# State scalings over all 128 partitions with a zero-padded scale table, and another order of work, in a retention and channel-mixer kernel

## The chip, the cores and the metric

The kernel runs on one core of one Trainium2 chip. The metric is the device time of one execution in microseconds (us), as the median of several runs; lower is better. A profile of one execution is read beside it. In the profile PE is the TensorE matmul engine, PEld its weight loads, DVE is VectorE, ACT is ScalarE, POOL is GpSimd and SP is SyncE, whose queue here only issues DMAs. "L434" is line 434 of the kernel file. In the changed file the same statements stand one or two lines further down.

## The reference

Two parts follow each other. The first is a retention layer: for each of 4 batches and 8 heads a 64x64 state decays by a constant gamma of the head at every one of 768 time steps, takes in an outer product of k and v, and is read by q. The second is a mixer over tokens and then over channels, with relu in between.

```python
def _attn_ref(q, k, v) -> np.ndarray:
    B, H, S, D = q.shape                      # 4, 8, 768, 64
    gamma = 1.0 - 2.0 ** (-5.0 - np.arange(H, dtype=np.float32))
    scale = 1.0 / np.sqrt(D)
    for t in range(S):
        state = gamma[None, :, None, None] * state + np.einsum('bhd,bhe->bhde', k[:, :, t], v[:, :, t])
        y[:, :, t] = scale * np.einsum('bhd,bhde->bhe', q[:, :, t], state)

def _moe_ref(x, w_tok1, w_tok2, w_ch1, w_ch2) -> np.ndarray:
    xt = x.transpose(0, 2, 1)
    h = np.maximum(xt @ w_tok1, 0.0) @ w_tok2        # 768 -> 256 -> 768
    u = x + h.transpose(0, 2, 1)
    h2 = np.maximum(u @ w_ch1, 0.0) @ w_ch2          # 512 -> 1536 -> 512
    return (u + h2).astype(np.float32)
```

## The kernel before

Time is cut into 6 chunks of 128 steps, and heads are taken in 4 pairs per batch, so that a pair fills 128 partitions (64 rows for each head). Work falls into a "front" for each batch and pair, and a "back" for each batch.

A front loads k, q and v of the pair by DMA, scales k and q by decays (L343 on ACT or L345 on DVE), turns them (PE transposes at L377 and L379, or DMA transposes issued by SP at L367, with the evictions L387 and L392), and forms two things. Scores within a chunk come from PE at L453 and are masked by DVE at L463 into the tile `am`. States between chunks come from PE at L408 into a bank, and DVE runs the recurrence over the five chunk ends at L418 and L420 into the tile `U` (128 partitions, 5 blocks of 64). The state is then scaled once more by the pair's decay over a chunk and written, as f16, into a tile `diag`, of 5 blocks of 128x128 that hold head 0 in the upper left quarter and head 1 in the lower right one, and zeros elsewhere (L434 on ACT, L436 on DVE; one instruction for each head). With it one full matmul per chunk (L483) serves both heads. PE adds both parts in a bank (L474 and L483), ACT or DVE evicts it (L489, the cast `x`), the token mixer follows (L503, relu at L512 or L514, L523), and the result is cast (`u`, L529), kept in f32 (`X`, L539) and turned into `uT` (PE at L568 with the eviction L575 for the first batch, and a DMA transpose issued by SP at L553 for the others).

A back does the channel mixer of a batch: `widen` (L606, relu at L622) and `narrow` (L746), or variants that save one product in eight by sums of blocks (L679 with evictions L691, L696 and L717; L820 and L830 with evictions L810 and L837, and sums at L784). Outputs leave at L761 and L862.

The three buffers of `diag` are one constant tile. It is set to zero once by a DVE memset (L233), and the scalings write only the diagonal quarters:

```python
rows = rows_of(j)                                   # 64 rows of head j
r, u, g = RS.tile[rows, :, rows], US.tile[rows], gp[rows, p:p + 1]
if e == "ACT":
    nc.scalar.activation(r, u, AF.Copy, scale=g)    # L434
else:
    nc.vector.tensor_scalar(r, u, g, None, ALU.mult)  # L436
```

`gp` holds the decay of pair p in column p, head 0 on partitions 0 to 63 and head 1 on the others, by eight memsets (L229, L230).

The order is a table. `PLAN` is a string that names, one after the other, each operation of the program, with the engine on which it runs where two can do it, and the PSUM bank that it takes; "+" and a digit stand for that many filler matmuls on a tile of zeros (L935), which compute nothing that is used. `placed` reads it, and each engine gets its instructions in that order. Engines run their queues in order and wait for each other by semaphores. DMAs of the POOL and SP queues are issued in the table's order too.

Of the kernel before, what the change touches and what calls it, by code (L numbers as in the profile page):

```python
# [8 lines left out]
FP = mybir.dt.float32  # L9
F16 = mybir.dt.float16  # L10
AF = mybir.ActivationFunctionType
ALU = mybir.AluOpType
# [9 lines left out]
class Op:  # L22
# [15 lines left out]
DIGITS = "0123456789abcdefghijklmnopqrstuvwxyzABCDEFGHIJKLMNOPQRSTUVWXYZ"  # L38

PLAN = (  # L40
    "0500040b0f01080702030d1h10a1i0+e1n01o1j1060e0h1p1q1k0+31l2091m+51w211z1v340c1y1r0g1S01T01s+61U41t01W01Y21u01V0"
    "1x1A1X+32x11Z0i2t026042021280j27352u0+62v02b1B52w0221C2y230m1E62401F250292a2z21D00k1G00l2H012J2K2A2B2c42C2D"
    "+12d2f32E2F12g+11H11I1J00n2I022L0p2M2N10r2e02h02G01N1K2i01L02j2k13412O1M02Q20q1O02R351385390E0w2P02l2S01P00o"
    "3602o2m03a63b3703c2T53d2U3e2n03i073k3L42V03f2p02q02W3j053l3g02r33o72Z3h03p1Q63n0t3m0u3M1R13r02X03003s3253q03t0"
    "2s03310x3u43v3H03w14k64l3114T50s5s44U3I03x3y02Y0aD33A3D2aA65t3B03J53F3E0aBaJ1aKaE3K13z13G0bj5aC3C00zaFaL3N7"
    "3V06243Z0v0Aba3bkbbbcb443Wbg03XbH1bIb5bE3bhbi3Y3O0y4g13PbF3Q3R4h10C3SbJb12b2b34i03T1431b77b8b6bG0D0Bbl4P14j1"
    "4u04260H4Q14xaY34w4R53U0aZaG2b0b9aS4aHaI444v0G40741aT4y4m24S14V5421466451bv347aV04W4n4Xbw480494c4o4paU0F4Y4q4Z"
    "4rbx500I19aP45353264a0aW4d14b0aM754aNaQ4z5555105204s04t11faO0Jbm3bnbd7aX4AaRbs456btbB2bKbp04e04B0by1bqbobCbzbr"
    "bebfbD4F01a575b65c4C3154DbM164E04f587bQ2171cbLbu4G4H00P595o15a0bO44IbA5d04LbP04J05e15f186114M0bR5p1bT5q2c6bN"
    "5u00K5v5g05w4K1bU05h5k5x5r0cc15i0ca55y5zbXcdc8bY10L4N05Y05Z05j05l05m060bV15C70325A0bW5G646655F0M5n5B0620bZc263"  # L50
    "5K3cb0ch266c74O0N7G05D5Ecfcs5L5H05I5J00Rcy7c0cuc3ci676869ctcvcg07H15M0cw15N45Ocj5P05Q5Tck00Oczc95R0cD45S06x1cl"
    "cocm1dce5U0cp5V0cE5W3cx06y0cB6D26EcC06FbS5X06c5076cHcF6dd356A1cI6B0cG0di47607820Q6g6a16zcO36C6GcP0ScU6cQcVd4"
    "6b1df3djdgd5dhcK6fd956e7716HdV3cJcW0VcL6h6dWd61d7dadb7a0dl01e6Idm6J16K17b17I26i6k5do26ldn1gdS7dTd00dpd86j06m0"
    "6n17c6o1bcndk6p1dqdXdUd1dx2dyd2dz6L71347K06P6N7d00W79du26tdv6q6O7L16r0cX1dD36M8k0dc4dd7edE6s1dF6u16v0de7f7g6T6"
    "6U7hc1dM7cY6Q3dw6R0U0TcR5cScAcZcTdYdN7N16S07i7OdZ7PdP2e06V0dQ6W56X6Y08l1dJ07MdKdLdO7J8Q1dR7Q7R7S726ZdG5700710"
    "7307j1dHdI7408g07T08R0e278h0e310X6w0Y7l12047oe437U07k0e7e57m7p8m7ne96eadr18Tds7V24307We817q57Z8jed7t2118S28i2"
    "dt7rdA17udBee7s0eb7v0dC7w6ec07x7y07Ye1eg8367X80481ef84eh8X7820eG8n17z7C863ek8U08508V1878YeI8o8Z7A0eM07B08808W"
    "898p7D090eNel8q7E08a0eK38ceq2eR0138b0eL0en8r8d0918s929308v7145eHeS8xer7FePeQ08w8yeVeW8t0eo28zemeO8e0ep0eT8u0et"
    "eu0eU1955064758f8A78Be6ex998C08D49697esey09q0ev1eweX8EeC9409r08F0eDez12eJeAf210cM1c41cq1fB0f62f78G58Hf3a00eB"
    "8I00ZeYfk1fCa22f85fafFc50f5eZflfof9fD3fbfGfd8Jfm59u0fp9v1cN0fI8Ma11fEfJf4frfc39wfe98fn8K0fq6fffsfy9a5fNcr0fO9t"  # L60
    "fifwfj14fgft9ba39c09s19d09efhfu9f1f11g62fvfAfxg79g3ei1eE19h8N09x19i09ya768L09za89Agaa9gk39j8O09BaafH4glgm79mgo"
    "9CfKgbabgnfLg81fP79k09l09n09o0fMacgpgd9F6405g9fz9Jgc1fQgefTgigrf00gq59G9D09HfR6fV49IfU9E09K09LgffSgjgs9M09N2fW"
    "fXgggtgy9Ogw9Q69P0gu9Ra41a50fYghad0g1fZg3gva6g4g09S09W9Tgx9U0gAg59V09X0g2gz8PgBgCgF3gXeF0h14gH0gG0af7561gDgIah"
    "gKh209Y0gM2agh30gL0ae0gNajgZgOak79palgYgQh81gP0am0aian6aogEgJap1h6aq5h0h9argT9Zh70as0atau0awgRhjh4gSh5haax0az"
    "hb0gUhlav0hchp0hfhu3hkhdhehvhFhJ1hKhn7hX5hYho1hqhh0ay0hyhGej1hshHi1hL6hZ0hghrhMhzie4ht0hwi2hx0hmi4hNhOig3hAi0"
    "hBhIhQhP0ifhRiiis6i32hSihi5hVi6hTichCijhWi9iahUi7iJ1itiy3iliX0i8ik2imiu5iYiwj1inioj2ixidipiKiqiZ7ibj0irj4iviz"
    "j5iL2iNj34iP5iMjbiOj9gW0hE1gV1iQiAjW2iEhi1iRj6iBj7jaiSiCkc0iTiFiGiDiIiVjcj8iUjdiHiWjejAjgjE3jF0ji6jXjYjZk0k1"
    "jG5jCjBhD0jL4jp1jJjj0jMjfjnjK0jNjo0jPjHjDk2jqjIk30jQjrjO0jSjRjtjU1jTkdk43kekfjV0js1kgkhjujvjhjk1jy1jwk5k6kijl"
    "kj0jmk7k8jxk9kajz0kb0"
)  # L70


# [24 lines left out]
def kernel(  # L97
# [11 lines left out]
    nc = tc.nc  # L109
    B, H, S, D = q.shape  # L110
# [58 lines left out]
    def either(emit, **costs):  # L169
        return [(e, c[0], c[1], lambda emit=emit, e=e: emit(e)) for e, c in costs.items()]  # L170
# [62 lines left out]
    diag_op = prep("DVE", 775, lambda: nc.vector.memset(diag, 0.0), prio=(-20, 0, -1, 2))  # L233
# [80 lines left out]
    def front(b, p):  # L314
# [19 lines left out]
        def rows_of(j):  # L334
            return slice(j * D, (j + 1) * D)
# [90 lines left out]
        for j in range(2):  # L426
            def emit(e, j=j):
                if RS.tile is None:
                    RS.tile = diag[:, rcount[0] % BUFS["r16"]]
                    rcount[0] += 1  # L430
                rows = rows_of(j)
                r, u, g = RS.tile[rows, :, rows], US.tile[rows], gp[rows, p:p + 1]
                if e == "ACT":
                    nc.scalar.activation(r, u, AF.Copy, scale=g)  # L434
                else:
                    nc.vector.tensor_scalar(r, u, g, None, ALU.mult)  # L436
# [531 lines left out]
```

## Time and profile before

| what | us |
|---|---|
| median of 3 runs | 188.86 (187.83 to 189.07) |
| the profiled execution, its own time | 187.85 |
| its span, first to last instruction | 186.1 |
| DVE busy, all of the span | 162.8 |
| ACT busy | 125.8 |
| POOL busy | 38.8 |
| granted TensorE clock | 1.00 throughout |

The span leaves out 1.75 us of the execution's own time. The busy time of an engine is the union of its instructions; matmuls overlap each other in the pipeline, so the distance from one matmul to the next says more than the duration of one. The prediction shows the rows that it uses.

### The profile page before, as it was taken

Reading aid. Unit: us, or ns where it says so; the run is one execution under the profiler, and the core shown is the slowest. Engines: PE = TensorE matmul, PEld = TensorE weight load, DVE = VectorE, ACT = ScalarE, POOL = GpSimd, SP = SyncE. Lnnn points to the kernel's source line nnn. Section 1 sums busy time; section 2 is a strip of 40 time slices with the busy share of each in tenths; the row PEclk is TensorE's granted clock in tenths of the full one; section 3 lists DMA queues with packets and bytes.
Section 4 is the critical chain, followed back from the end, with each engine's and each line's share of the span. In section 5 each row is a group of like instructions: output and inputs, shape, how many; then the busy total and the mean of one; then the engine's idle time right before and its main releaser. Section 6 shows DMA issues by size and latency. Waiting matters only on the chain.

```text
span 186.1 us, 5220 instructions
## 1 busy us (share of the span) xinstructions
PE 179.2 (96%) x2079; PEld 135.2 (73%) x2079; DVE 162.8 (88%) x424; ACT 125.8 (68%) x288; POOL 38.8 (21%) x49
## 2 busy tenths in 40 slices
PE   7889999899999999999999999999999999999993
PEld 3556888567679898667677888767678987656882
DVE  5589889689999999995889899989999999789882
ACT  3768898654969948557789677889986435774100
POOL 8994199373015000101003000010000000000000
PEclk9999999999999999999999999999999999999999
DMA  8999999999999999399999799979528031231044
GB/s 114 151 166 202 175 184 185 167 193 206 179 154 158 148 113 224 79 176 230 228 181 138 176 168 216 309 191 226 194 45 187 0 99 62 86 139 58 4 181 157
DMA packets 94233, 29.05 MB, mean 156 GB/s; under 512 B 84352, under 2 KB 91264, under 8 KB 94208
## 3 DMA queue, kind: packets, MB, share of 16 engines
q0 software_dynamic: 39520, 9.64, 54.1%
q1 hardware_dynamic: 52816, 15.93, 47.5%
q10 hardware_dynamic: 1872, 3.15, 4.7%
q8 instruction: 16, 0.26, 0.6%
q14 instruction: 9, 0.07, 0.2%
HBM read 26.74 MB, written 6.29 MB: 178 GB/s over the span
## 4 chain that ended last, share of the span: by engine, by line
PE 81%; ACT 7%; DVE 4%; DMA 3%; POOL 2%; issue 1%; POOLq 0%; DVEq 0%; ACTq 0%
PE bank L820 16%; PE bank L606 15%; PE bank L679 15%; PE bank L830 12%; PE bank L503 5%; PE bank L523 5%; DMA row<-in_k_dram 3%; PE bank L453 3%; PE bank L746 3%; PE bank L474 3%; PE bank L483 2%; ACT diag L434 2%; DVE am L463 2%; PE bank L408 1%; DVE U L420 1%; ACT X L539 1%
## 5 line engine op out<-in xcount | busy, mean ns | idle before, releaser
L606 PE MATMUL bank<-uT,wc 128*128 128x384 f16 x192 | 36.3, 326 | 0.7 <-ACT uT L575 0.6
L463 DVE TENSOR_TENSOR am<-bank,mask 128x384 f16<-128x384 f32 x64 | 32.8, 550 | 3.9 <-PE bank L453 3.7
L622 ACT ACTIVATE h<-bank 128x384 f16<-128x384 f32 x48 | 21.3, 497 | 9.5 <-PE bank L606 9.3
L606 PEld LDWEIGHTS <-wc 128*128 128x128 f16 x192 | 17.4, 98 | 9.8 <-issue 0.9
L696 DVE TENSOR_TENSOR h<-bank,us 128x384 f16<-128x384 f32 x36 | 19.1, 552 | 2.4 <-PE bank L679 1.6
L691 ACT COPY us<-bank 128x384 f32<-128x384 f32 x36 | 16.4, 487 | 6.6 <-PE bank L679 5.1
L820 PEld LDWEIGHTS <-hs 128*128 128x128 f16 x198 | 18.8, 98 | 2.6
L837 DVE TENSOR_TENSOR X<-X,bank 128x256 f32<-128x256 f32 x44 | 18.0, 415 | 2.4 <-PE bank L830 2.1
L810 ACT COPY us<-bank 128x256 f32<-128x256 f32 x27 | 10.1, 380 | 14.1 <-PE bank L820 13.1
L820 PE MATMUL bank<-wsum,hs 128*128 128x256 f16 x132 | 17.5, 273 | 0.0
L420 DVE SCALAR_TENSOR_TENSOR U<-U,gp,bank 128x64 f32<-128x64 f32 x64 | 16.4, 276 | 0.9
L360 POOL CAST v<-row 128x768 f16<-128x768 f32 x5 | 4.1, 827 | 61.5 <-DMA row<-in_v_dram 53.0
L529 ACT CAST u<-bank 128x384 f16<-128x384 f32 x30 | 14.6, 499 | 2.7 <-PE bank L523 2.6
L489 ACT CAST x<-bank 128x384 f16<-128x384 f32 x28 | 12.9, 485 | 3.7 <-PE bank L483 3.5
L679 PE MATMUL bank<-hs,wsum 128*128 128x384 f16 x72 | 15.3, 326 | 0.0
L523 PE MATMUL bank<-h,wt 128*128 128x128 f16 x192 | 14.5, 219 | 0.0
L503 PE MATMUL bank<-x,wt 128*128 128x128 f16 x192 | 14.2, 219 | 0.2 <-ACT x L489 0.2
L539 ACT COPY X<-bank 128x384 f32<-128x384 f32 x28 | 14.0, 503 | 0.1
L434 ACT ACTIVATE diag<-U,gp 64x320 f16<-64x320 f32 x24 | 13.3, 559 | 0.9 <-DVE U L420 0.4
L830 PEld LDWEIGHTS <-h 128*128 128x128 f16 x132 | 12.3, 98 | 1.8
L503 PEld LDWEIGHTS <-wt 128*128 128x128 f16 x192 | 12.0, 98 | 2.1 <-issue 0.6
L523 PEld LDWEIGHTS <-wt 128*128 128x128 f16 x192 | 12.1, 98 | 1.9 <-issue 0.2
(91 smaller groups left out, 364.3 us busy)
## 6 DMA issues: line engine op xcount, KB each, us to landing
out_dram<-X SPq DMA_DIRECT2D x12, 256.0 KB, 2.8
out_dram<-X ACTq DMA_DIRECT2D x11, 256.0 KB, 2.2
wc<-in_moe_w_ch_dram POOLq DMA_DIRECT2D x5, 512.0 KB, 13.0
row<-in_k_dram SPq DMA_DIRECT2D x6, 384.0 KB, 5.2
row<-in_q_dram SPq DMA_DIRECT2D x6, 384.0 KB, 5.0
row<-in_v_dram SPq DMA_DIRECT2D x6, 384.0 KB, 4.6
v<-in_v_dram POOLq DMA_DIRECT2D x10, 192.0 KB, 8.3
row<-in_q_dram POOLq DMA_DIRECT2D x10, 192.0 KB, 8.1
```

Of the source, the lines that this page charges most:

```text
L420: nc.vector.scalar_tensor_tensor(out=u[:, c], in0=u[:, c - 1], scalar=gp[:, p:p + 1], in1=st, op0=ALU.mult, op1=ALU.add)
L434: nc.scalar.activation(r, u, AF.Copy, scale=g)
L463: nc.vector.tensor_tensor(am, SC[g].tile[:, :m * P].rearrange("p (i t) -> p i t", t=P), mask.to_broadcast([P, m, P]), ALU.mult)
L503: nc.tensor.matmul(acc[:, jt * P:(jt + 1) * P], wt1[:, i, jt * P:(jt + 1) * P], X16.tile[:, i], start=(i + jt == 0), stop=(i == NC - 1), s ...
L523: nc.tensor.matmul(Y[hf].tile[:, i * P:(i + 1) * P], wt2[:, jt, t], H1.tile[:, jt], start=False, stop=(jt == NJ - 1), skip_group_check=True)
L606: nc.tensor.matmul(acc[:, :SH], wc1[:, ct, ft * P:(ft + 1) * P], UT.tile[:, ct, sh * SH:(sh + 1) * SH], start=(ct == 0), stop=(ct == NP - 1))
L622: nc.scalar.activation(H2.tile[:, ft], A.tile[:, :SH], AF.Relu)
L679: nc.tensor.matmul(acc[:, :SH], left(ct), r[:, ct], start=first and ct == 0, stop=ct == 1, skip_group_check=True)
L696: nc.vector.tensor_tensor(into(hf)[:, ft], bank.tile[:, :SH], kept(j), ALU.add)
L820: nc.tensor.matmul(acc_[:, lo], l[:, j], r[:, j], start=first and j == 0, stop=j == K2 - 1, skip_group_check=True)
L830: nc.tensor.matmul(acc_[:, lo], l[:, j], r[:, j], start=first and j == 0, stop=j == K2 - 1, skip_group_check=True)
L837: (nc.vector if e == "DVE" else nc.gpsimd).tensor_tensor(dst(), dst(), b_(), ALU.add)
```

## The change

There are three edits.

1. A table `gz` of 128 x 2 x 4 numbers: column (j, p) holds the decay of head j of pair p in that head's 64 partitions and zero in the other 64. It is made by one memset to zero and eight memsets of 64 partitions. `gp` is now the sum of the two halves (one DVE add of 128x4).
2. A scaling now reads all 128 partitions of `U`, multiplies by column (j, p) of `gz`, and writes all 128 rows of head j's 64 columns in each of the five blocks: its own quarter, and zeros in the quarter of the other head's rows. So every write makes the zeros anew, and the memset of `diag` (L233) and its place in the dependencies are gone.
3. `PLAN` is another string. It holds 32 fillers where there were 39, and moves work between engines: of the scalings 7 instead of 8 of the 32 run on DVE.

```diff
+    gz = const_p.tile([P, 2, NP], FP, name="gz")
...
     def emit():
+        nc.vector.memset(gz, 0.0)
         for p in range(NP):
-            nc.vector.memset(gp[:D, p:p + 1], g128[2 * p])
-            nc.vector.memset(gp[D:, p:p + 1], g128[2 * p + 1])
-    gp_op = prep("DVE", 770, emit, prio=(-20, 0, -1, 2))
-
-    diag_op = prep("DVE", 775, lambda: nc.vector.memset(diag, 0.0), prio=(-20, 0, -1, 2))
+            for j in range(2):
+                nc.vector.memset(gz[j * D:(j + 1) * D, j, p:p + 1], g128[2 * p + j])
+        nc.vector.tensor_tensor(gp, gz[:, 0], gz[:, 1], ALU.add)
+    gp_op = prep("DVE", 960, emit, prio=(-20, 0, -1, 2))
...
-                rows = rows_of(j)
-                r, u, g = RS.tile[rows, :, rows], US.tile[rows], gp[rows, p:p + 1]
+                r, u, g = RS.tile[:, :, rows_of(j)], US.tile, gz[:, j, p:p + 1]
...
-            rs.append(op(either(emit, ACT=(460, 557), DVE=(458, 536)), [prev, diag_op] + rs, [] if rs else [RS],
+            rs.append(op(either(emit, ACT=(460, 557), DVE=(458, 536)), [prev, gp_op] + rs, [] if rs else [RS],
...
 PLAN = (
-    "0500040b0f01080702030d1h10a1i0+e1n01o1j1060e0h1p1q1k0+31l2091m+51w211z1v340c1y1r0g1S01T01s+61U41t01W01Y21u01V0"
+    "040007030a050e01020c091g01h1+e1m01n1i1061o1p080d1j00b+31k2+21V11q1r1l1s11t01v201u341y0g1R00f1z1S01W+51D0+11T2"
```

The first place is the start of DVE's queue. Before, the exponents `lgs`, which ACT needs for the decays of k, are ready ahead of the memset of `diag` and the table `gp`:

```order
L928 MEMSET zero 128x192
L219 MEMSET lnh 64x1 x8
L198 MEMSET lgs 128x1 x8
L199 MEMSET lnsc 128x1
L200 TENSOR_SCALAR lgs<-lgs,away 128x8
L233 MEMSET diag 128x960
L229 MEMSET gp 64x1
L230 MEMSET gp 64x1
```

In the changed kernel the same stretch of DVE's queue, up to the first scaling of k (the tile `k_128`), reads:

```order
L929 MEMSET zero 128x192
L229 MEMSET gz 128x8
L232 MEMSET gz 64x1 x8
L233 TENSOR_TENSOR gp<-gz 128x4
L209 TENSOR_SCALAR ident_75<-away 128x128
L220 MEMSET lnh 64x1 x8
L199 MEMSET lgs 128x1 x8
L200 MEMSET lnsc 128x1
L201 TENSOR_SCALAR lgs<-lgs,away 128x8
L347 TENSOR_SCALAR k_128<-us,gk 128x6x64
```

The memset of `diag` is gone, `gz` and the sum `gp` come first, and `lgs` moved from the front of the list to its end.

The second place is the end of the first batch's fronts. In ACT's queue before, the two halves of pair 3 are cast (`u_772`), and both evictions of the turned tile (`uT`, out of bank_785) stand on ACT too, right ahead of the first relus of the back:

```order
L343 ACTIVATE k_716<-row,gk 128x6x64 x2
L529 CAST u_772<-bank_643 128x384
L539 COPY X<-bank_453 128x3x128
L529 CAST u_772<-bank_677 128x384
L575 COPY uT<-bank_785 128x384 x2
L622 ACTIVATE h_821<-bank_789 128x384
```

In the changed kernel the cast of the first half (`u_779`) and both evictions (out of bank_788) stand in DVE's queue, among the scaled turns `qT` of the next batch:

```order
L540 COPY X<-bank_440 128x3x128
L389 TENSOR_TENSOR qT<-bank_722,gq 128x768
L530 CAST u_779<-bank_665 128x384
L389 TENSOR_TENSOR qT<-bank_634,gq 128x768
L576 COPY uT<-bank_788 128x384 x2
L347 TENSOR_SCALAR k_785<-row,gk 128x6x64
```

The last evictions of the batch left ACT for DVE, and the second cast (`u_779` out of bank_685) stays on ACT behind a copy `X`. On PE the work around them moved too. Before, PE's queue has three matmuls of `widen` (L606) between the halves of pair 3's second token product (L523), then the first three turns of `u_772`, three more of `widen`, the six turns of `k_716` (L379), the last three turns of `u_772`, and then `widen` on the tile that waits for those turns. In the changed kernel both halves of the token product follow each other, then come nine matmuls of `widen`, all six turns of `u_779`, and three more matmuls of `widen` that don't need them; the turns of k of the next batch come later.

The third place is the last front, pair 3 of batch 3. Before, both casts of its result (`u_3101`) stand in ACT's queue right behind the relu `h_3093` of its token mixer, and SP's DMA transpose of `u_3101` reads them:

```order
L512 ACTIVATE h_3093<-bank_3070 128x256
L529 CAST u_3101<-bank_3022 128x384
L529 CAST u_3101<-bank_3051 128x384
L810 COPY us<-bank_2949 128x256
L539 COPY X<-bank_3022 128x3x128
```

In the changed kernel the second cast of that result (`u_3128`, out of bank_3054) stands in DVE's queue, at the end of this stretch:

```order
L785 TENSOR_TENSOR hs<-h_2627 128x768 x2
L838 TENSOR_TENSOR X<-X,bank_3090 128x256
L838 TENSOR_TENSOR X<-X,us 128x256
L540 COPY X<-bank_3040 128x3x128
L530 CAST u_3128<-bank_3054 128x384
```

The cast moved from ACT, where it followed the relu at once, to DVE behind two sums, two additions and a copy. In SP's queue an output DMA (L863), which reads the result of the second of these additions, now stands ahead of the transpose of `u_3128`.

POOL's DMA queue issues the same loads. Two loads of batch 0 are swapped (q of pair 2 ahead of v of pair 1), and of batch 1 all four q come ahead of the first k, with the first two pieces of the channel weights among them.

More of the change, by code (lines that the diff above doesn't have):

```diff
@@ L46 @@
[L46 to L60, printed above, removed]
@@ L66 @@
[L66 to L69, printed above, removed]
+    "040007030a050e01020c091g01h1+e1m01n1i1061o1p080d1j00b+31k2+21V11q1r1l1s11t01v201u341y0g1R00f1z1S01W+51D0+11T2"
+    "2w11w1U00h1x1A42s026232x2a1X51Y1Z1E25162t0+52u3282v00i0l20272y61B292z0j21+12G322A2B222H151C01F00k2C2302I2402D"
@@ new lines @@
+    "4q4a05n1bl0bm4bbw4X523517bn4c0aO64Y5o14d04Z5450155184r00Gb00b14y50H53565p2b34b4aP4s0b2510aQ0Ib54ebA0bc3bd4z4A0"
+    "bx6be5745q158bBbybJbL4B3bC5a24C4E0bK5b5t74D0bz0J0K4F4G0141615175u5905c0c50ObN6bO0cb04K4H4I05d1cc5ebSbP06005v"
+    "5f04L05gc75wbQ4M04J0bT05x5ybMbU35h05i0bVbW5j5X1bX15Y06105B4705626315E0L5Fc6c1bYc9564ca05z05C5Dc2bZ5A0c8cr5J0"
+    "cv4cect5G30P5k05Hcs65cf06667195Kcw05I0685L05Zcu6w1cx6ci5M7cj15NcA6z15O05P5Q05mcdcB05ScC1cg76A04NcEcnch6x15R0"
+    "5T0cF1ckbRcyco5U05l0cl5V27900M6y6b56036C7cJcD5W0cG7a11d7506ecK6ccH6DcN0cO6Edk46f1a6dde5dR10Ncm7F0dldSdfcPdh0dg"
@@ new lines @@
+    "6906Bd866F6a1d96g5dn3dodi6hda760dp6G6j6cZ26i10QcT36HcIdjdT6kcUcVdmd216m70Vd0d36l16nd47G17716o1d54d67bd10R"
+    "6K71307c2d76I06p6L6q07J16N6OdU4cQ7dV6r07d7edF37K1dW6J00Sc07fdGdb0dc6scW47H2cR6McXdHcS6t0dI17gdddt3du6S7dv6T6P0"
+    "6u07h6Q7IdC27i11f7M36R0cYdz67N6U1786V56vdD7O6WdE6X08f0dq4dAdX0XdJ7P1bdBdYe06YdZe157QdKdr8g16Z0700dsdw1dxe207R"
+    "8P07S1717Lcz720730dy7k34060Ue6e328T07o8U07T07j0dL17n7l7me4dO0dPdQe717U4376dM8j07X0Te827s77W0W7p0e5e97q8k17r07V"
+    "ea7tec8Q17u0c31108i7Y8led7Z4dNeF807v37web0ef7x0ee7y7BeJ3eHejeL28268108R1837z07A0eK07C0eg7D0840eM8W58h28m0857eG"
@@ L70 @@
+    "jAjfjK0k0jIjLjGji1jJ0jo3k1jpjejOjgjCk21jMjmjN0jn0jPjQjT1jsk30jqjr0jtjujj5jRjvjSjHjkkb3kcjlkdjx1jwjU0jy1kekfk4"
+    "k5k6kgkhk7ki0k8k9ka0"
 )
```

24 lines of the change are left out of this document (15 added, 9 removed).

## The prediction

> **What bounds the kernel now.** I read the page first, then busy times by stretches, then who PE waited for, then the timeline where PE was short of work. The rows below are the page's busy times of PE, and four stretches (bounds and length in us, busy us with instructions of PE, PEld, DVE, ACT and POOL, then clock, DMA share and GB/s).
>
> ```profile
> PE 179.2 (96%) x2079; PEld 135.2 (73%) x2079; DVE 162.8 (88%) x424; ACT 125.8 (68%) x288; POOL 38.8 (21%) x49
> ...
> 5.80:18.10 12.30, 10.97 (x173) 7.46 (x173) 9.98 (x24) 9.03 (x16) 9.62 (x12) 1.00 1.75 175
> 18.10:30.40 12.30, 11.91 (x235) 10.04 (x233) 10.63 (x27) 11.29 (x26) 8.00 (x10) 1.00 1.74 178
> 30.40:33.40 3.00, 2.47 (x32) 1.96 (x31) 3.00 (x6) 1.96 (x6) 2.98 (x4) 1.00 1.53 195
> 33.40:182.90 149.50, 149.16 (x1632) 113.74 (x1631) 135.48 (x340) 100.59 (x238) 13.09 (x14) 1.00 0.97 154
> ```
>
> From 33.4 us to its last matmul PE is busy 149.16 of 149.5 us. In the stretches ahead busy time overstates, since the length of a small matmul covers the gap to the next (the part on the end of the fronts shows it). After 36 us the list of PE's waits has one row, and the chain that ended last closes with one eviction, after which one output leaves:
>
> ```profile
> PE bank L503 <- ACT x L489: 0.2, 1, 0.2
> ...
> 182.96 0.42 DVE X L755
> ```
>
> So a new order can win almost nothing after 33.4 us (0.34 us idle at most) and can lose there; the matmuls that count stay the same, and both orders end on the same eviction and output. The gain must come from the first 33 us.
>
> **The start.** Rows of the timeline: start, length, engine, line, and in brackets the idle time before with what ended it.
>
> ```profile
> 2.06 0.51 DVE L200 TENSOR_SCALAR lgs<-lgs,away 128x8 f32<-128x8 f32 x1
> 2.43 0.86 DVE L233 MEMSET diag<- 128x960 uint32 x1
> 2.60 0.21 ACT L204 ACTIVATE gk<-lgs 128x8 f32<-128x8 f32 x1 [0.59 <-DVE lgs L200]
> 4.54 0.61 ACT L343 ACTIVATE k<-us,gk 128x384 f16<-128x384 f32 x1 [1.53 <-DMA us<-in_k_dram]
> 4.54 0.66 DVE L345 TENSOR_SCALAR k<-us,gk 128x384 f16<-128x384 f32 x1 [0.33 <-DMA us<-in_k_dram]
> 6.16 0.48 PE L408 MATMUL bank<-v,k 128*64 128x64 f16 x10 [0.37 <-DMA v<-in_v_dram]
> ```
>
> The memset of 0.86 us is gone, but DVE waits 0.33 us for the first k even with it, and PE's first product waits for v until 6.16. Added are a memset of 128x8 and an add of 128x4, which no row shows: between 0 and, by the memset above and `lgs` (0.51, also a few columns), 0.86 and 0.51; I take 0.1 and 0.5. DVE is then done about 4.21 - 0.86 + 0.6 = 3.95, and since `lgs` is now last in its list, `gk` ends near 4.2 instead of 2.8, still ahead of k at 4.54. With the upper ends it would be 0.5 us late, and the scalings of k, done at 5.2, have 0.96 us before PE can use them. Cost and gain: 0, covered by the loads of k and v.
>
> **The scalings.** Groups by shape: busy us, mean ns of one, idle before.
>
> ```profile
> L434 ACT ACTIVATE diag<-U,gp 64x320 f16<-64x320 f32 x24 | 13.3, 559 | 0.9 <-DVE U L420 0.4
> L436 DVE TENSOR_SCALAR diag<-U,gp 64x320 f16<-64x320 f32 x8 | 4.3, 538 | 0.2
> L345 DVE TENSOR_SCALAR k<-row,gk 128x384 f16<-128x384 f32 x4 | 1.7, 414 | 0.0
> ```
>
> With 128 partitions the free size stays 320. On ACT the nearest row is the scaling of k at 4.54: 128 partitions, 384 columns, 610 ns, so length follows columns and not partitions: 559 again (bounds 0.51, that row by 320/384, and 0.61). On DVE the bounds are 0.345 (the third row by 320/384) and 0.66 (the 128-partition scaling at 4.54). Which end? The 64-partition row is the slow one, 1.68 ns a column against 1.08. I take 538 again: the five blocks have not changed. All 32 then cost what they did; the lower DVE end would save 7 x 0.19 = 1.3 us of DVE, nearly all after 33.4 us where DVE does not bound. The Trainium skill (page "VectorE: DVE Perf Modes", section on Mode 2×_2P) says that one-source operations in SBUF run two elements a cycle only if the outermost count is even, or equal on both sides; five blocks out of one run of 320 would stay slow and the six blocks of k are fast, and by that rule as by my choice the sum gets 0.
>
> **Fillers.** Seven fewer, and all 39 stood before 18.4 us (the group with its first and last start, then two of its stretches):
>
> ```profile
> L935 PE MATMUL bank<-zero x39: 326/326/528, 1.1 to 18.1; 128*128 128x384 f16 x39
> ...
> 1.12 4.66 PE L935 MATMUL bank<-zero 128*128 128x384 f16 x14 [1.12 <-DVE zero L928]
> 10.00 1.15 PE L935 MATMUL bank<-zero 128*128 128x384 f16 x6
> ```
>
> The distance of two is (1.15 - 0.33)/5 = 0.164 us, so 1.15 us of PE work goes. PE has 12.3 - 10.97 = 1.3 us idle in that stretch and waits for k, q and the masks anyway; worth 0.
>
> **When pair 3's second token product starts.** DVE waits early, and again just before it reaches k of pair 3 at 22.03. With it stand the groups of this stretch on ACT, and one DVE group:
>
> ```profile
> 8.55 0.96 DVE L387 TENSOR_TENSOR qT<-bank,gq 128x768 f16<-128x768 f16 x1 [0.74 <-PE bank L377]
> ...
> 21.69 0.42 DVE L514 TENSOR_SCALAR h<-bank 128x256 f16<-128x256 f32 x1 [0.54 <-PE bank L503]
> 22.03 0.54 DVE L345 TENSOR_SCALAR k<-row,gk 128x384 f16<-128x384 f16 x2
> ...
> L529 ACT CAST u<-bank 128x384 f16<-128x384 f32 x30 | 14.6, 499 | 2.7 <-PE bank L523 2.6
> L489 ACT CAST x<-bank 128x384 f16<-128x384 f32 x28 | 12.9, 485 | 3.7 <-PE bank L483 3.5
> L512 ACT ACTIVATE h<-bank 128x256 f16<-128x256 f32 x13 | 5.1, 393 | 5.2 <-PE bank L503 5.2
> L784 DVE TENSOR_TENSOR hs<-h 128x768 f16<-128x768 f16 x18 | 9.6, 552 | 1.2 <-ACT h L622 0.9 <-PE bank L820 0.3
> ```
>
> The new order puts two casts `x` and a cast `u` in front of that k (0.55 each on DVE, by the last row, which is near the 0.5 on ACT) and takes the relu of 0.42 away: +1.23. It has the idle 0.74 and 0.54 to fill, the first with two steps of the recurrence that stood later. The loads up to pair 3 are the same but for one swap. So the product starts at 30.38 as before, within -0.5 (the idle time, with nothing put in) and +1.2 (nothing filled). POOL's loads of batch 1 put two q and two weight pieces (0.2 and 0.26 MB each) ahead of the first k; at 178 GB/s it lands 5 us later, after 31 us. PE's turns of that k moved behind twelve L606: 0, at most 0.5.
>
> **The end of the fronts.** PE's rows around it, and the ACT eviction that it waits for:
>
> ```profile
> 30.38 0.51 PE L523 MATMUL bank<-h,wt 128*128 128x128 f16 x6
> 30.73 0.65 PE L606 MATMUL bank<-uT,wc 128*128 128x384 f16 x3
> 31.22 0.50 PE L523 MATMUL bank<-h,wt 128*128 128x128 f16 x6
> 31.55 0.33 PE L568 MATMUL bank<-ident,u 128*128 128x128 f16 x3
> 31.72 0.65 PE L606 MATMUL bank<-uT,wc 128*128 128x384 f16 x3
> 32.21 0.50 PE L379 MATMUL bank<-ident,k 128*128 128x128 f16 x6
> 32.54 0.33 PE L568 MATMUL bank<-ident,u 128*128 128x128 f16 x3
> 32.91 0.86 ACT L575 COPY uT<-bank 128x384 f16<-128x384 f16 x2 [0.68 <-PE bank L568]
> 33.44 1.46 PE L606 MATMUL bank<-uT,wc 128*128 128x384 f16 x8 [0.57 <-ACT uT L575]
> ```
>
> By distances (0.163 us for 384 columns, (1.46 - 0.33)/7; 0.058 for 128, (0.51 - 0.22)/5) PE does 12 x 0.058 + 6 x 0.163 + 12 x 0.058 = 2.37 us of work in these 3.06 us: 0.69 us lost. In the new order nine L606 (1.47 us) follow the product, while ACT and DVE cast `u` (0.5 us each); then the six turns (0.35) and three more L606 (0.49), during which DVE, behind a `qT` of 0.95 us, begins the evictions. The last eviction then ends up to 0.25 us after PE wants it. Gain: 0.69 - 0.25 = 0.45 (bounds 0 and 0.69).
>
> **Batch 3's last front.** The new place of the cast adds a wait for the DMA transpose. Rows: the two casts before, the transpose, its landing times over the run, a DVE group now ahead of the second cast (with L784 above), and one PE step of the back.
>
> ```profile
> 148.03 0.86 ACT L529 CAST u<-bank 128x384 f16<-128x384 f32 x2 [0.61 <-PE bank L523]
> 148.92 1.21 SPq L553 DMA_TRANSPOSE uT<-u  x1
> ...
> DMA to landing us min/median/max: 2.7/4.2/7.7
> ...
> L837 DVE TENSOR_TENSOR X<-X,bank 128x256 f32<-128x256 f32 x44 | 18.0, 415 | 2.4 <-PE bank L830 2.1 <-PE bank L820 0.2
> ...
> 155.52 0.66 PE bank L820 x6
> ```
>
> From the token product's end PE has seven such steps and two products of 0.33 ahead of the first that needs the tile: 7 x 0.66 + 0.65 = 5.27 us. DVE needs 2 x 0.55 + 2 x 0.42 + 0.55 (copy) + 0.55 (cast; L529 on DVE, as L784) = 3.04, the transpose 2.7 at its fastest: 5.74. So 0.47 us is missing if DVE starts its stretch at the product's end, 0 if it is ahead by that much; before, the transpose was issued 0.9 us after the casts began, so it had over 2 us more. SP's queue holds an output in front, ready before the cast. I take 0.25, half of it (0 to 2.0, at the median landing).
>
> **The sum.** 187.85 (the profiled execution: span 186.1 and 1.75 around it) + 0 + 0 + 0 + 0 - 0.45 + 0.25 = 187.65. The runs shown have a median 1.0 above that execution, and their lowest equals it; a new median should lie between the two, so I say 187.65 + 0.45 = 188.1 us, -0.4% of 188.86. A measurement of this kernel can tell about 1% from no change.
>
> **Rivals.**
> A, slower: the transpose of batch 3. It shares the DMA queues with outputs, and the column of landing times reaches 7.7. PE waits by as much as landing exceeds 5.27 - 3.04 = 2.23 us, and all products of batch 3's back stand behind. At the median of 4.2 that is 2.0: 188.1 - 0.25 + 2.0 = 189.85; above 190.75 it decides from 5.1 us to landing on. Against it: the transposes issued alone, as the one at 148.92, are near the minimum.
> B, faster: the first 33 us are bound by DVE and ACT and not by loads. Up to the last eviction of the first fronts the new order has on ACT two `u`, two `x` and the two evictions of 32.91 less, two relus and one copy (0.5, as `u`) more: -1.0 - 0.97 - 0.86 + 0.79 + 0.5 = -1.54. On DVE, where these casts went, two `qT` and a `kT` of the next batch come later: -1.9 - 0.55 for +2.2 of casts, +0.8 of evictions, -0.84 of relus and -0.27 of a k: -0.6. If PE is full earlier by their mean, 1.1, and the whole 0.69 goes without A's wait: 188.1 - 1.1 - 0.24 - 0.25 = 186.5. For it: ACT is busy 11.29 of 12.3 us. Against it: DVE waited just before pair 3's k.
> C, slower: with fewer fillers PE falls back to the pace of its first 14 matmuls, (4.66 - 0.33)/13 = 0.333 us each, twice the later distance. Between 5.8 and 18.1 us there are 10.97 - 25 x 0.164 = 6.9 us of other work at most; a third of the stretch at half pace costs 2.3, less a third of the idle time and of the 18 fillers left there, (1.33 + 2.95)/3 = 1.4: 189.0; all of it 190.7. The Trainium skill (page "TensorE: Matmul & The Clock Gate", Part 1) states that the array falls to half its clock after about 3.4 us of idling; the change of pace after the first 14 agrees with it, and it speaks against taking fillers away.
>
> **Chances.** My forecast 0.55 (same 0.47, faster 0.04, slower 0.04); A 0.20 (same 0.10, slower 0.10); B 0.18 (faster 0.14, same 0.04); C 0.07 (same 0.04, slower 0.03). That makes faster by over 1% (below 186.97) 0.18, within 1% 0.65, slower by over 1% (above 190.75) 0.17. The range takes in B's 186.5 and A's 189.85, and reaches past that for landings above the median: 186.2 to 190.6.
>
> **What would show it.** Scalings at 128x320 near 559 and 538 ns; the first product again near 6.16; PE's last wait in the fronts below 0.3 us instead of 0.57, and full use from about 33 us; a transpose of the last `u` issued over 3 us after its product, with a wait of PE under 0.5. I am wrong if scalings on DVE or ACT take twice as long, if PE's waits after 36 us add up to over 2 us, or if full use comes before 32 us.

## The result, and the profile after

The changed kernel takes 185.71 us in the median of 6 runs (185.40 to 186.28), the kernel before, run beside it, 188.04 (187.11 to 189.07). The ratio is 0.987 with a 95% interval of 0.984 to 0.990: faster by 1.3%. The forecast was 188.1 with a range from 186.2, so the time lies on the side of rival B and below the range. The profiled execution took 185.76 us, with a span of 184.0 (before 187.85 and 186.1). Here and below, ratios leave out the few runs far above the others of a kernel, as one of 207 us at a granted clock of 0.85.

The page's row of PE, and then the busy times by the stretches that the prediction used (columns as there), of the changed kernel:

```profile
PE 177.9 (97%) x2072; PEld 134.7 (73%) x2072; DVE 163.3 (89%) x427; ACT 122.9 (67%) x287; POOL 38.0 (21%) x48
```

```profile
5.80:18.10 12.30, 10.68 (x163) 6.75 (x164) 11.34 (x30) 8.52 (x16) 9.79 (x12) 1.00 1.74 175
18.10:30.40 12.30, 12.30 (x254) 11.11 (x251) 10.09 (x23) 10.27 (x25) 7.79 (x10) 1.00 1.80 181
30.40:33.40 3.00, 3.00 (x23) 1.84 (x22) 2.38 (x6) 2.31 (x6) 3.00 (x4) 1.00 1.80 182
33.40:180.80 147.40, 147.27 (x1628) 113.01 (x1625) 136.07 (x339) 99.02 (x238) 12.29 (x14) 1.00 0.94 156
```

ACT changed most in the stretch from 18.1 to 30.4 us: it is busy 10.27 us and not 11.29. DVE is busy 10.09 and not 10.63 there, and PE, which was busy 11.91 of 12.30, is full. The stretch after 33.4 us is as full as before. The timeline of the changed kernel's PE at the end of batch 0's fronts shows where the head ends:

```profile
29.38 0.84 PE L524 MATMUL bank<-h,wt 128*128 128x128 f16 x12
30.06 1.63 PE L607 MATMUL bank<-uT,wc 128*128 128x384 f16 x9
31.52 0.50 PE L569 MATMUL bank<-ident,u 128*128 128x128 f16 x6
31.86 2.72 PE L607 MATMUL bank<-uT,wc 128*128 128x384 f16 x15
```

Pair 3's second token product starts at 29.38 us instead of 30.38, and the product that waits for the last turned tile has no wait worth a row (it was 0.57 us, at 33.44). From that token product to the end of the last matmul it is 151.4 us (29.38 to 180.76), where it was 152.5 (30.38 to 182.92). The matmuls on either side of it are the same in number and shape, but for the seven fillers. So 1.0 us comes from the time ahead of it and 1.1 from behind it.

The groups of the scalings by shape, changed kernel:

```profile
L435 ACT ACTIVATE diag<-U,gz 128x320 f16<-128x320 f32 x25 | 13.5, 580 | 0.0
L437 DVE TENSOR_SCALAR diag<-U,gz 128x320 f16<-128x320 f32 x7 | 3.8, 540 | 0.1
```

580 and 540 ns stand where the prediction had 559 and 538. By these means nothing was won, and that is where the prediction was led astray: the next rows show why a mean duration doesn't tell it. They are ACT's timeline around the pair of scalings of batch 0's pair 3, the kernel before first, then the changed one.

```profile
25.98 1.15 ACT L434 ACTIVATE diag<-U,gp 64x320 f16<-64x320 f32 x2
27.15 0.86 ACT L529 CAST u<-bank 128x384 f16<-128x384 f32 x2
```

```profile
25.56 1.01 ACT L435 ACTIVATE diag<-U,gz 128x320 f16<-128x320 f32 x2
26.48 0.46 ACT L530 CAST u<-bank 128x384 f16<-128x384 f32 x1
```

From the start of the first to the start of what follows the second it was 27.15 - 25.98 = 1.17 us, 0.585 each, and is now 26.48 - 25.56 = 0.92, 0.46 each. In the kernel before, a scaling of head 1 on ACT begins 12 to 26 ns after the instruction ahead of it has ended, and so does what follows it (13 to 30 ns), unless that is of head 1 too; around scalings of head 0 an instruction mostly starts about 100 ns before its neighbour ends. Over 128 partitions all scalings on ACT overlap like that. Each change of the half that an instruction starts on costs about 0.12 us of ACT.

### The profile page after: what moved, and what is told of

It reads as the page before. It is cut to its first block, busy times and chain, and to the rows that moved or that the text cites. A ratio compares the mean times of both kernels' runs of the same rounds, so it can differ in the third digit from the quotient of the medians.

```text
span 184.0 us, 5212 instructions
## 1 busy us (share of the span) xinstructions
PE 177.9 (97%) x2072; PEld 134.7 (73%) x2072; DVE 163.3 (89%) x427; ACT 122.9 (67%) x287; POOL 38.0 (21%) x48
## 3 DMA queue, kind: packets, MB, share of 16 engines
q1 hardware_dynamic: 53104, 16.46, 45.9%
## 4 chain that ended last, share of the span: by engine, by line
PE 87%; DMA 4%; DVE 4%; POOL 3%; ACT 1%; issue 0%; DVEq 0%; POOLq 0%
PE bank L821 16%; PE bank L607 16%; PE bank L680 15%; PE bank L831 12%; PE bank L504 6%; PE bank L524 6%; DMA row<-in_k_dram 4%; PE bank L475 3%; PE bank L454 3%; PE bank L747 3%; PE bank L484 2%; PE bank L410 2%; PE bank L381 1%; POOL v L297 1%; POOL row L294 1%; PE bank L379 1%
## 5 line engine op out<-in xcount | busy, mean ns | idle before, releaser
L623 ACT ACTIVATE h<-bank 128x384 f16<-128x384 f32 x48 | 22.7, 500 | 9.4 <-PE bank L607 9.0
L697 DVE TENSOR_TENSOR h<-bank,us 128x384 f16<-128x384 f32 x36 | 18.4, 548 | 1.3 <-ACT us L692 0.7
L422 DVE SCALAR_TENSOR_TENSOR U<-U,gp,bank 128x64 f32<-128x64 f32 x64 | 17.0, 282 | 0.8
L362 POOL CAST v<-row 128x768 f16<-128x768 f32 x4 | 3.4, 838 | 63.5 <-DMA row<-in_v_dram 41.3
L680 PE MATMUL bank<-hs,wsum 128*128 128x384 f16 x72 | 14.5, 326 | 0.0
L831 PEld LDWEIGHTS <-h 128*128 128x128 f16 x132 | 12.8, 98 | 1.6
L490 ACT CAST x<-bank 128x384 f16<-128x384 f32 x26 | 11.8, 488 | 3.1 <-PE bank L484 3.1
L838 DVE TENSOR_TENSOR X<-X,us 128x256 f32<-128x256 f32 (+1 forms) x22 | 13.1, 605 | 0.8 <-ACT us L811 0.5
L435 ACT ACTIVATE diag<-U,gz 128x320 f16<-128x320 f32 x25 | 13.5, 580 | 0.0
L680 PEld LDWEIGHTS <-wsum 128*128 128x128 f16 x96 | 9.2, 98 | 5.7
```

The lines of the kernel that those rows point to most:

```text
L422: nc.vector.scalar_tensor_tensor(out=u[:, c], in0=u[:, c - 1], scalar=gp[:, p:p + 1], in1=st, op0=ALU.mult, op1=ALU.add)
L623: nc.scalar.activation(H2.tile[:, ft], A.tile[:, :SH], AF.Relu)
L680: nc.tensor.matmul(acc[:, :SH], left(ct), r[:, ct], start=first and ct == 0, stop=ct == 1, skip_group_check=True)
L697: nc.vector.tensor_tensor(into(hf)[:, ft], bank.tile[:, :SH], kept(j), ALU.add)
L831: nc.tensor.matmul(acc_[:, lo], l[:, j], r[:, j], start=first and j == 0, stop=j == K2 - 1, skip_group_check=True)
L838: (nc.vector if e == "DVE" else nc.gpsimd).tensor_tensor(dst(), dst(), b_(), ALU.add)
```

## The experiments

All times below are medians, with the lowest and highest run. Kernels in the old order scatter by 1 to 4 us, those in the new order mostly by 1; ratios are to the kernel before on the same chip.

**Scalings and order apart.** Scalings alone keeps the old `PLAN`; order alone keeps the old scalings, the old `gp` and the memset:

```diff
 # scalings alone: the changed kernel, with
-PLAN = (the new string)
+PLAN = (the string before)
 # order alone: the kernel before, with the new string, and in it, behind DVE's first scaling of k
+    nc.vector.memset(diag, 0.0)
```

> The changed scalings and the table gz, with no memset of diag, in the order of the kernel before with its 39 fillers. Theory (the gain of 2.3 us is the order's; scalings cost what they did): within 0.4 us of the kernel before, about 188.0 us, ACT scalings of 128x320 near 565 ns and DVE ones near 538 ns. Rival 1 (the gain is the missing memset and the full-width scalings): 185.7 to 186.5 us. Rival 2 (they cost something and the order pays for it): 188.7 us or more.

> The new order with its 32 fillers, but the scalings of 64 partitions, the table gp by eight memsets, and the memset of diag, now behind DVE's first scaling of k, where DVE waits 1.0 us for PE. Theory: 185.7 us, within 0.4 of the changed kernel. Rival 1 (scalings carry the gain): 187.5 to 188 us. Rival 2: under 185.2 us.

Measured: scalings alone 187.82 us (186.94 to 189.94), ratio 0.9985 (0.9956 to 1.0014); order alone 187.01 (186.49 to 187.38), ratio 0.9924 (0.9896 to 0.9951). So the first theory held and the second did not: the order gives about half, and the new order with the old scalings is 1.3 us slower than with the new ones, while in the old order the same scalings are hardly worth anything. Both were run once more later, with the expectations

> The changed scalings in the order before, once more beside these: theory A ratio 0.994, theory B 0.9985.

> The new order with scalings of 64 rows and the memset, once more beside these: ratio 0.9925 (0.990 to 0.995), 187.0 us.

and gave 187.58 us, ratio 0.9961 (0.9926 to 0.9997), between the two theories, and 186.95, ratio 0.9919 (0.9888 to 0.9949). The changed kernel itself was run again too:

> The changed kernel itself, beside the two above on the same chip: 185.4 to 186.0 us, ratio 0.986.

It took 185.45 us (185.00 to 187.22), ratio 0.9859 (0.9811 to 0.9908).

**Fillers.** Seven more in the changed kernel, seven fewer in the one before:

```diff
 # counts of the groups, in the order in which they stand
-14, 3, 2, 5, 1, 5, 1, 1   (changed)
+14, 3, 5, 6, 2, 6, 2, 1
-14, 3, 5, 6, 3, 6, 1, 1   (before)
+14, 3, 2, 4, 3, 4, 1, 1
```

> The changed kernel with its 7 fillers back (3 more behind the first turns of q, 1 each in two other places and 2 in two pieces, all before 17 us). Theory as predicted (before 18 us PE waits for loads, a filler is free): 185.7 us, within 0.3. Rival 1 (each filler costs its 0.163 us, so that 1.14 of the 2.1 us of span are the fillers'): 186.8 us. Rival 2 (fillers keep PE fast, more are better): under 185.4 us.

> The kernel before with 7 of its 39 fillers taken out (3, 2 and 2 from the groups at 8.4, 10.0 and 14.0 us). Theory (free): 188.0 us, within 0.4. Rival 1 (each costs its price): 186.9 us. Rival 2 (PE falls to a slower pace without them): 189 us or more.

Measured: 185.59 us (185.14 to 185.99) with 39 in the new order, 187.66 (186.99 to 189.62) with 32 in the old one, ratio 0.9979 (0.9948 to 1.0011). A filler ahead of 18 us is free, and seven fewer don't slow PE down. Rival C falls.

**What it is about the scalings.** In the third kernel both scalings of a pair start on partition 0, with 64 rows and the memset, so that only the change of the start is taken away:

```diff
 # order alone, with
-r, u, g = RS.tile[rows, :, rows], US.tile[rows], gp[rows, p:p + 1]
+r, u, g = RS.tile[:D, :, rows_of(j)], US.tile[:D], gp[:D, p:p + 1]
```

> New order, memset of diag as in order alone, and scalings of 64 rows that all start on the same half: both heads' columns are filled from the first 64 rows, so the lower half of the blocks stays zero and head 1's result is left out. Theory (the change of the start costs, not the number of rows, nor the memset): ACT's scalings follow each other at 0.46 us as in the changed kernel, and the time is the changed kernel's, 185.7 us (185.4 to 186.1). Rival 1 (64 rows are what keeps them apart, or the memset costs): 187.0 us; with distances of 0.46 us and 187.0 us it would be the memset.

It took 185.41 us (184.93 to 186.05). ACT's timeline at the four scalings that the new order puts in a row, with the cast `x` behind them, for order alone, the changed kernel and this one:

```profile
17.12 2.29 ACT L433 ACTIVATE diag<-U,gp 64x320 f16<-64x320 f32 x4
19.43 0.48 ACT L488 CAST x<-bank 128x384 f16<-128x384 f32 x1
```

```profile
17.19 1.92 ACT L435 ACTIVATE diag<-U,gz 128x320 f16<-128x320 f32 x4
19.01 0.46 ACT L490 CAST x<-bank 128x384 f16<-128x384 f32 x1
```

```profile
16.96 1.92 ACT L432 ACTIVATE diag<-U,gp 64x320 f16<-64x320 f32 x4
18.78 0.46 ACT L487 CAST x<-bank 128x384 f16<-128x384 f32 x1
```

From the first scaling to the cast it is 2.31, 1.82 and 1.82 us: 0.58, 0.455 and 0.455 each. With one start 64 rows are as fast as 128, and the memset, which stands in this kernel too, costs nothing. So it is the change of the start and neither the number of rows nor the zeros. The Trainium skill (page "VectorE: DVE Perf Modes", section "Two Vector instructions with no wait between them") states such a rule for VectorE: an instruction whose input or output starts in another quadrant of 32 partitions than the last input or output in the same memory starts only when all before it have finished. DVE agrees with it here, as two rows of the changed kernel's start show, one of eight memsets that go from half to half and one of eight that don't:

```profile
2.57 0.75 DVE L220 MEMSET lnh<- 64x1 f32 x8
3.37 0.12 DVE L199 MEMSET lgs<- 128x1 f32 x8
```

0.094 us each against 0.015. These differ in their rows too, but DVE's scaling of 64 rows late in batch 3 does not: to the next instruction it takes 0.56 us in order alone, where it starts on another half than its neighbours (142.86 to 143.42), and 0.45 in the third kernel, where it doesn't (140.85 to 141.30). The runs show the same on ACT. The Trainium skill (page "ScalarE: Activation LUTs", section "What ACT_TABLE_LOAD costs") gives about 93 ns by which ACTIVATEs in a row overlap; the 0.565 us that the median scaling lasts in the changed kernel less the 0.455 from one to the next, 0.11, agree with that.

**Where it counts.** The wide scalings in batch 0 only, and everywhere but in batch 0:

```diff
+if b == 0:      # the other kernel: if b > 0
     r, u, g = RS.tile[:, :, rows_of(j)], US.tile, gz[:, j, p:p + 1]
+else:
+    rows = rows_of(j)
+    r, u, g = RS.tile[rows, :, rows], US.tile[rows], gp[rows, p:p + 1]
```

> The changed kernel, but only the eight scalings of batch 0 are over 128 partitions; those of batches 1 to 3 are over 64 rows again (the three buffers keep the zeros of batch 0). Theory (a scaling that starts on another half of the partitions than its neighbour waits until that one has ended, 0.12 us at each such change; the loss is PE's only where nothing covers it, and in batch 0 the scalings stand on the path, 0.65 us later at pair 3's second token product): about half of the 1.3 us between order alone (187.0) and the changed kernel (185.7) comes back, 186.3 us (186.0 to 186.6). Rival (all of it is lost in batch 0's fronts): 185.7 us. Rival (all later): 187.0 us.

> The complement: new order, table gz and the memset of diag behind DVE's first k; batch 0 scales over 64 rows and batches 1 to 3 over 128 partitions. Theory: 186.4 us (186.1 to 186.7). Rival (all of it is lost in batch 0's fronts): 187.0 us. Rival (all later): 185.7 us.

Measured: 185.95 us (185.74 to 186.30) and 186.21 (185.97 to 186.69). The first lies just under its expected range, the second in it. Batch 0's eight scalings are worth 0.5 us (186.21 against 185.71) and the 24 later ones 0.24; against the changed kernel's run on the same chip (185.45) it is 0.76 and 0.50, which adds up to the 1.3 that both together cost. Which of the two is nearer the truth these runs can't tell. In batch 0 one sees it in the start of pair 3's second token product: 30.05, 30.57 and 29.67 us in the three profiles of the new order with narrow scalings there, 29.01 to 29.38 in the six without the crossing. With pair 3's k landing at the same time, it is 29.67 with the crossing (k at 21.26) and 29.15 in the second profile of the changed kernel (k at 21.24).

**The end of batch 0's fronts.** Put back in the new order, as rows of the table:

```diff
 # PE, behind the first half of pair 3's second token product
-second half, widen x9, turns of u x6, widen x3
+widen x3, second half, turns of u x3, widen x3, turns of u x3, widen x6
 # cast of the first half, both evictions of the turned tile
-DVE
+ACT
```

> The changed kernel with the end of batch 0's fronts as before: the casts and both evictions of pair 3's turned tile on ACT, three products of widen between the halves of the second token product, and the turns in two groups of three. Theory (the prediction's term for this place): PE waits again for the last eviction, 0.4 to 0.7 us, 186.3 us (186.1 to 186.5). Rival (the place gives nothing of its own, since later work waits for other things): 185.7 us.

It took 186.32 us (186.13 to 186.99), 0.6 more than the changed kernel's first median and 0.9 more than its second: the place carries what the prediction gave it or more (0.45). The loss is not one wait for the last eviction, as the theory had it. No wait of PE behind 28 us is long enough to be listed; from the start of each half of the token product to the next matmul it is 0.57 us, where six such matmuls take 0.35, and the wait for the last eviction is about 0.2. Taking it into the old order was harder. There, in a first try, the turns of the next batch's k were the cover behind the six turns, and in a second three products of `widen`, with the eviction of `kT` ahead of the last `qT`:

```diff
 # the kernel before: PE behind the first half, first and second try
+second half, widen x9, turns of u x6, turns of k x6, widen
+second half, widen x6, turns of k x6, turns of u x6, widen
 # cast of the first half, both evictions
-ACT
+DVE
```

> The kernel before with one place of the new order: at the end of batch 0's fronts both halves of pair 3's second token product stand together, nine products of widen follow, then the six turns, then the turns of k of the next batch as cover; one cast and both evictions of the turned tile are on DVE. Scalings as before. Theory (putting this place back cost 0.6 us in the new order, so it gives as much in the old one): 0.5 to 0.7 us under the kernel before, ratio 0.9965 (0.9955 to 0.998), and PE's wait of 0.57 us there is gone. Rival (in the old order other work is late next, the gain is given back): ratio 0.999 to 1.001.

> The same with the scalings over 128 partitions, the table gz and no memset of diag. Theory (in the old order the pair of scalings ahead of pair 3's casts gives 0.25 us, and the scalings later little): 0.8 to 1.0 us under the kernel before, ratio 0.995 (0.994 to 0.9965). Rival (with that place mended the scalings are worth what they are in the new order, 1.3 us): ratio 0.990 or less.

> The kernel before with the end of batch 0's fronts as in the new order, now with the eviction of the next batch's kT on DVE ahead of the last qT, and three products of widen behind the six turns as cover. Theory: both waits (0.57 us as before, and the 0.9 us for kT of the first attempt) are under 0.2 us, and the time is 0.4 to 0.7 us under the kernel before, ratio 0.997 (0.9955 to 0.9985). Rival (given back later): ratio 0.999 to 1.001.

> The same with the scalings over 128 partitions and no memset of diag. Theory A (the scalings are worth as much in the old order as between the two runs of the first attempt): 1.0 to 1.2 us under the kernel with the place alone, ratio to the kernel before 0.991. Theory B (in the old order they give the 0.25 us ahead of pair 3's casts and little more): 0.2 to 0.5 us under it, ratio 0.995.

Measured: the first try 188.22 us, ratio 0.9982 (0.9958 to 1.0007), with wide scalings 187.14, ratio 0.9920 (0.9891 to 0.9949); the second 189.23, ratio 1.0043 (1.0008 to 1.0078), with wide scalings 187.93, ratio 0.9973 (0.9941 to 1.0006). PE's waits in the second, from 28 us on, say why:

```profile
PE bank L378 <- DVE qT L386: 0.8, 1, 0.8
PE bank L407 <- DVE X L538: 0.8, 1, 0.8
```

The wait of 0.57 us is gone, but PE now waits for two PSUM banks that DVE empties later than before, since evictions that stood on ACT are ahead of them. In the first try it was one bank, for 0.9 us. These four tell nothing of the place's worth in the old order; they show only that these parts of it, taken over alone, bring other waits. Between the two of each pair the wide scalings gave 1.1 and 1.3 us, as theory A had it or a little more, while in the untouched old order they gave 0.15% and 0.4%, 0.3 to 0.7 us.

**Why the old order scatters.** In the second profile of scalings alone PE lost 2.0 us at one place. Its list of waits from 33 us on, and DVE's rows there:

```profile
PE bank L380 <- DVE k L346: 2.0, 1, 2.0
PE bank L606 <- ACT uT L575: 0.6, 1, 0.6
```

```profile
57.96 0.32 DVE L346 TENSOR_SCALAR k<-row,gk 128x384 f16<-128x384 f16 x1 [2.61 <-DMA row<-in_k_dram]
58.20 0.95 DVE L904 TENSOR_TENSOR wsum<-wc,wsum 128x1536 f16<-128x1536 f16 x1
59.06 0.31 DVE L346 TENSOR_SCALAR q<-row,gy 128x384 f16<-128x384 f16 x1
59.30 0.41 DVE L837 TENSOR_TENSOR X<-X,bank 128x256 f32<-128x256 f32 x1
59.63 0.32 DVE L346 TENSOR_SCALAR k<-row,gk 128x384 f16<-128x384 f16 x1
```

It is k of batch 1's pair 3. In the old order POOL issues its load at 39.0 us, behind the last piece of the channel weights and the q of batch 2's first pair, and it lands 16.5 us later, at 55.5, in the profile of the kernel before. DVE scales the second half of that k at 57.84 there, behind a sum of the weights, and PE uses it at 58.65:

```profile
56.19 0.31 DVE L345 TENSOR_SCALAR k<-row,gk 128x384 f16<-128x384 f16 x1
56.42 0.95 DVE L904 TENSOR_TENSOR wsum<-wc,wsum 128x1536 f16<-128x1536 f16 x1
57.28 0.32 DVE L345 TENSOR_SCALAR q<-row,gy 128x384 f16<-128x384 f16 x1
57.52 0.42 DVE L837 TENSOR_TENSOR X<-X,bank 128x256 f32<-128x256 f32 x1
57.84 0.44 DVE L345 TENSOR_SCALAR k<-row,gk 128x384 f16<-128x384 f16 x1
...
58.65 0.50 PE L379 MATMUL bank<-ident,k 128*128 128x128 f16 x6
```

So even in that execution, one of the shortest of its kernel, it was 58.65 - 57.84 - 0.44 = 0.37 us from a wait. Not every gain ahead of it is given back here, though. In the profile of the old order with 32 fillers pair 3's second token product starts 0.76 us earlier (29.62 us), this load lands at 54.73, and the next second token product behind this place is still 0.76 us earlier (58.60 against 59.36). In the second profile of scalings alone the load was issued at 39.68, landed only at 57.94, and that product came at 60.72. How much of the scatter is this place's was not shown. The new order issues this load at 32.65 us, it lands 13.3 later, at 46.0, and DVE scales the k at 46.64 and 47.38. Three kernels moved parts of this into the old order: the load alone, the load with wide scalings, and DVE's scaling of this k as well, ahead of the sums:

```diff
 # POOL's loads, all three kernels
-wc x3, q of batch 2 pair 0, v and k of batch 1 pair 3
+wc, k and v of batch 1 pair 3, wc x2, q of batch 2 pair 0
 # DVE, the third kernel
-four sums of wc, k first half, sum of wc, q, X, k second half
+k both halves, five sums of wc, q, X
```

> The kernel before, with the loads of k and v of batch 1's pair 3 moved ahead of the last two pieces of the channel weights and of q of batch 2's pair 0 in POOL's queue; nothing else. Theory (in the old order this load is the second bound: it lands 0 to 2.4 us too late, and a gain ahead of it is given back there): it lands near 46 to 48 us instead of 55.5 to 57.9, PE never waits at the turns of that k, the times lie within 1.2 us of each other, and the median is 0.4 to 1.0 us under the kernel before, ratio 0.996 (0.9945 to 0.998). Rival (the scatter comes from elsewhere): ratio 0.999 to 1.001 with a scatter of 2 us or more.

> The same loads, with the scalings over 128 partitions and no memset of diag. Theory (with the load out of the way the scalings give in the old order what they give in the new one, 0.6 to 1.3 us): ratio 0.990 (0.988 to 0.993), 0.6 to 1.3 us under the run with the loads alone. Rival (the old order hides the scalings, whatever the load): less than 0.4 us under it.

> The order before with full-width scalings and the early load of batch 1's pair 3, and now DVE scales that k ahead of the first sum of the channel weights (which waits for their last load), as the new order does. Theory: PE's wait of 1.25 us at the turns of that k is gone, the median is 1.5 to 2.5 us under the run without this move (189.5), 187.0 to 187.9 us, ratio to the kernel before 0.992 to 0.998, and the times lie within 1.2 us. Rival (the loss is elsewhere, PE's wait moves to the next product that needs the sums): 188.8 us or more.

Measured: 189.40 us (188.20 to 191.36), ratio 1.0027 (0.9993 to 1.0061); 189.48, ratio 1.0028 (0.9993 to 1.0062); and 187.99, ratio 0.9976 (0.9949 to 1.0002). The first two theories failed: the load lands at 45.9 and 46.1 us, as expected, but neither the time nor the scatter falls, and the wide scalings give nothing. The load alone doesn't help, since the last piece of the weights now comes later and DVE's queue stands still for it, with the scaling of k behind it. The row of DVE in the load-alone kernel, and of PE:

```profile
52.88 0.96 DVE L903 TENSOR_TENSOR wsum<-wc 128x1536 f16<-128x1536 f16 x1 [1.29 <-DMA wc<-in_moe_w_ch_dram]
...
59.41 0.51 PE L378 MATMUL bank<-ident,k 128*128 128x128 f16 x6 [1.27 <-DVE k L344]
```

With the k scaled ahead of the sums the time falls by 0.5% (1.0 us, by the ratios) to 1.5 us (by the medians), but PE still waits 0.60 us at the same turns, now for the bank that the addition L837 behind the same sums has to empty. So the place is DVE's queue from 50 to 59 us, with two loads in it, and not the one load. The expectation for the third kernel was narrowly missed in the median and missed in the wait, which moved as its rival had it, though the time did not stay where the rival had it.

## Why the prediction was wrong

**The bound.** Right that PE is full from some 33 us on and that the head decides. For the two profiled executions it is right too that almost nothing is won after 33.4 us: PE is idle 0.34 us there before and 0.13 after. But it was read from one execution, the fastest of three, which met its load in time with 0.37 us to spare; the two profiles of scalings alone lose 0.5 and 2.0 us there at single places. The scatter of the runs shown (187.83 to 189.07) was in the table, and was taken for a spread that the new kernel would share (the 0.45 us added to 187.65). The new kernel has 185.40 to 186.28, and 185.00 to 187.22 when it was run again.

**The start.** Right: `gk` runs at 4.05 us, and nothing of the missing memset shows. The first product starts at 5.72 us, not near 6.16, and that is v's landing: in the twenty profiles of all kernels, with the memset or without, it starts 0.04 to 0.11 us behind it, between 5.60 and 6.16.

**The scalings.** This is the step that failed most. That all 32 "cost what they did" was taken from mean durations (559 ns on ACT, between 510 and 610, and 538 on DVE), although the same prediction priced PE's matmuls by their distance and not by their duration. By distance a scaling on ACT falls from 0.58 to 0.455 us when it crosses from one half of the partitions to the other or follows one that does. The row of the pair (1.15 us for two, and 1.17 to the next instruction) stood in the trace of before. In the new order this is worth 1.3 us (187.0 to 185.7), of a forecast of 0.

**Fillers.** Right: 0. The pace that rival C feared does not come back: five fillers in a row at 9.53 us of the changed kernel take 0.99 us, (0.99 - 0.33)/4 = 0.165 each. The rule of the Trainium skill that it went by (page "TensorE: Matmul & The Clock Gate", Part 1: half the clock after about 3.4 us of idling) was not put to the test, since PE is never idle for more than 1.2 us in either profile.

**Pair 3's second token product.** The prediction looked at DVE and at the load of k, and gave it -0.5 to +1.2 us. It came 1.0 earlier, and part of that is luck: the load landed at 21.15 us instead of 21.81, by no work of the kernel's. In four other profiles of the old order with narrow scalings it landed at 20.85 to 21.57, and the product starts at 29.62 to 29.88, so that 29.01 to 29.38 is earlier by 0.2 to 0.9 us. The order alone gives nothing of it, since with narrow scalings in batch 0 it starts the product at 29.67 to 30.57 us; nor do wide scalings in the old order (29.55 to 29.91 in six profiles). In the new order six scalings stand on ACT's queue ahead of the last casts `x`, four in a row and a pair, and they are 0.49 and 0.25 us shorter. Rival B had the right engine and the wrong reason: it counted casts moved off ACT.

**The end of the fronts.** Right in kind, 0.45 forecast, 0.6 to 0.9 measured.

**Batch 3's last front.** Too pessimistic: 0.25 forecast, 0 measured. The second cast starts at 147.84 us and SP issues the transpose at 148.45; it lands in its shortest time:

```profile
L554 SPq DMA_TRANSPOSE uT<-u x1: 1217/1217/1217, 148.5 to 148.5; - x1
...
DMA to landing us min/median/max: 2.7/2.7/2.7
```

That is 151.2 us, and by the prediction's count of PE's work (5.27 us, from 146.66 on, when the token product's last matmul has been issued) the tile is wanted at 151.9. DVE was ahead by more than the 0.47 us that were missing: its two sums L785, the first of the five steps counted, began at 145.47. Rival A falls with it.

**The sum again.** The forecast was 188.1 us. Less 1.3 (scalings), 0.15 (end of the fronts, 0.6 against 0.45), 0.25 (the wait for batch 3's transpose) and 0.45 (the scatter) it is 185.95, against the measured 185.71. The terms come from separate kernels and need not add up. What late loads cost the old order in a typical run, and how much of the order's gain is their removal, was not settled: the old-order kernels built to remove them each met another wait.

## What to carry to other kernels

Price an instruction by the distance to the next one on its engine when nothing is waited for, on every engine, and compare that with its duration: a gap above zero where its neighbours overlap is a cost that no mean shows. Two half-width instructions that go from one half of the partitions to the other can cost more than two full-width ones with zeros. And a profile is one execution: before saying that a saturated engine leaves nothing to win, look at the scatter of the runs and at how close each late load came to being waited for.

## What the runs showed of the hardware

On ACT an ACTIVATE that starts on another half of the partitions than the one before it begins 12 to 30 ns after that one's end, where others overlap it by about 0.1 us; 64 rows with an equal start overlap as 128 do (0.455 us from one to the next for 320 columns). On DVE the same crossing makes memsets of one column 0.094 us apart instead of 0.015, and makes a scaling take 0.56 us to the next instruction instead of 0.45. The same load of k (batch 1, pair 3), issued at 38.5 to 39.7 us by kernels in the old order, took from 15.0 to 18.3 us to land.
